# Slopes transformed at another place, conversions two at a time, one PSUM pool: a sparse-attention kernel with two MLP layers on one core

## The chip, the cores and the metric

The kernel runs on one core of a Trainium2 chip. The metric is device time in microseconds (us) of one execution. The engines are named as in the profile: PE (TensorE matmul), PEld (its weight loads), DVE (VectorE), ACT (ScalarE), POOL (GpSimd) and SP (SyncE, which issues nearly all DMAs here; its issues are listed as SPq).

## The reference

Three parts in sequence, all in float32 at the outside:

```
scores = (q @ k^T) / 8              # 4 batches x 8 heads, 576 x 576, head size 64
keep a score if it is >= row maximum - tau, else it counts as -1e9
attn   = exp(scores - max) / sum    # softmax over what is kept
x      = attn @ v                   # heads side by side: 2304 tokens x 512
h      = x @ w_in;  g = max(h, 0) + alpha * min(h, 0);  x = g @ w_out      # layer 1, 512 -> 2048 -> 512
h      = x @ w_in2; g = h > 0 ? h : exp(min(h, 0)) - 1; out = g @ w_out2   # layer 2, same sizes
```

The weights reach the chip as float64 bit patterns (loaded as 64-bit integers) and have to be turned into float32 there. `alpha` holds one slope for each of the 2048 hidden units of layer 1.

## The kernel before

**Stages.** Attention takes the first 364 us of the profiled execution, layer 1 the time from 364 to 778 us, layer 2 the rest. Every matmul of the MLPs works on values split into a high and a low part (`hi`, `lo = x - hi`), three products for one.

**Order of the work.** Every compute instruction goes through `pe`, `dve`, `act` or `pool` (class `Pinned`), which keeps each engine in the order in which the program was written. That order comes from time tables: a step is put down with a due time (`put(at, step)`), all steps are sorted by it and written out (`run`). So a step that waits holds up everything behind it on its engine. In attention the unit of due time is a job (one head's 128 rows of scores; `AT` gives the stages of a job relative to its number), and `beside(i)` is called every 1.3 jobs. In the MLPs the unit is about half an `h` or `o` block of layer 1 (12 matmuls of 128x128 by 128x384), as `sequence` lays them out: a chunk of 384 tokens takes 64 units, `begin` (layer 2's start) is at unit 384.

**Attention.** For each job: scores on PE into a double bank (pool `ps_s`, 3 buffers), row maximum on DVE (`top`), exponential on ACT, masking with the sum on DVE, scaling on POOL, transposes on PE into pool `ps_t` (2 banks), copies out on ACT. `prep(u, i)` transposes the next unit's k and q on PE. Units of q and k are loaded by SP in `load_unit`. Ahead of the first job stand, unpinned, a few DVE instructions: two on `tau` (lines 842 and 843), and line 846, which turns the slopes into 1 - alpha in place after line 845 has loaded them.

**Conversions.** A group (`groups`) is one 128-wide block of a layer-1 weight matrix, or two blocks of a layer-2 matrix (which are also combined into the seven operands of a Strassen-like product and stored to DRAM). `single()` makes one float32 block `x` in three steps: two ACT copies (`x<-r`, `t<-r`), then three DVE operations with a POOL addition at the end (`x<-x,t`). `conversion(g)` continues: for a layer-1 block the high part (from block 10 on ACT, `w<-x`) and the low part (DVE, `w<-x,w`). Both are Python generators; `convert_step` advances the one open conversion by one step. During attention 20 of the 32 layer-1 groups are converted. The other 12, two for each of the blocks 10 to 15, are due during layer 1's first chunk at 0.85 units a step (5 steps a group), and the 16 layer-2 groups (13 steps each) after that, spread evenly up to 8 units before `begin`:

```
    for i in range(4 * KFF):
        put(0.85 * i + 0.45, convert_step, len(groups))
```

**Layer 1.** `hidden_block(c, f)` multiplies (PE into tag `h`, pool `ps_h`, 4 banks), then ACT `t<-psh`, DVE `g<-t,alpha,psh`, ACT `gh<-g`, DVE `gl<-g,gh`. `outer_block` multiplies these two blocks later (LAG = 2) into the four banks of pool `ps_a`. At a chunk's end `result` copies the four banks to tiles `o` (2 buffers), which SP stores to `y`.

**Between the layers.** The last chunk's `outer_block` frees weight tiles in turn: of blocks 0 to 3 for layer 2's weights, of blocks 4 to 9 for its operands (`xs_of`, five 384-column blocks to a tile). `operand_steps(n)` loads `y`, makes the seven operands for each half `kb` of the depth, and splits them. `operand` says in which blocks one operand lies: the two halves of one product side by side. Then the pools `staging` and `first_layer` are closed, and pool `mlp2` (left side of SBUF) and pool `ps_8` (all 8 banks) are opened (lines 900 to 906).

**Layer 2.** `first_product` takes products in `IN_ORDER` 1, 2, 6, 7, 5, 3, 4; the third of them accumulates on the bank of the first, after ACT has copied that out (`keep`, tile `c`). `psum()` hands out banks in rotation over eight.

Of the kernel before, what the change touches and what calls it, by code (L numbers as in the profile page):

```python
# [20 lines left out]
def sparse_attention_two_mlps(  # L21
# [13 lines left out]
    nc = tc.nc  # L35
# [140 lines left out]
    def conversion(g):  # L176
        layer, part, p = group = groups[g]
        if layer == 0:
            for x in single():
                yield  # L180
            if part == 0:
                wt[p] = new_block(p)
            hi, lo = wt[p][:, part, 0, :], wt[p][:, part, 1, :]
            high_of(dve if p < FIRST else act, hi, x)
            if p >= FIRST:
                yield
            difference(dve, lo, x, hi.bitcast(F32))
            stored.add(group)
            return
        xs = []  # L190
        for _ in range(2):
            for x in single():
                yield
            xs.append(x.rearrange("p (a m) -> p a m", a=2))
        (a11, a12), (a21, a22) = [[x[:, h] for h in range(2)] for x in xs]
        if part == 1:
            a12, a21 = a21, a12
        s = stage.tile([P, 4, HM], F32, tag="s", name="s", bufs=1)
        s1, s2, s3, s4 = (s[:, n] for n in (0, 1, 2, 3))
        made = [((1, 2) if part == 0 else (1,), xs[0]), ((4,) if part == 0 else (2, 4), xs[1]),  # L200
                ((5, 6), s[:, 0:2]), ((7, 3), s[:, 2:4])]
        made[1] = (made[1][0], xs[1][:, 2 - len(made[1][0]):2])
        split = {}

        def high(n):
            products, of = made[n]
            split[n] = stage.tile([P, 2, 2, HM], F32R, tag="split", name="split", bufs=2)
            high_of(act, split[n][:, 0:len(products), 0, :], of[:, 0:len(products)])

        def low(n):  # L210
            products, of = made[n]
            many = len(products)
            difference(dve, split[n][:, 0:many, 1, :], of[:, 0:many],
                       split[n][:, 0:many, 0, :].bitcast(F32))

        def store(n):
            for i, product in enumerate(made[n][0]):
                to = in_d[p][:, IN_ORDER.index(product)] if part == 0 else out_d[product - 1][:, p]
                nc.sync.dma_start(out=to, in_=split[n].bitcast(F32)[:, i])
            split.pop(n)  # L220

        total(dve, s1, a21, a22)
        high(0)
        yield
        low(0)
        difference(dve, s2, s1, a11)
        high(1)
        yield
        low(1)
        difference(dve, s4, a12, s2)  # L230
        store(0)
        yield
        difference(dve, s3, a11, a21)
        high(2)
        store(1)
        yield
        low(2)
        high(3)
        yield
        low(3)  # L240
        store(2)
        yield
        store(3)
        stored.add(group)

    converting, started = [], [0]

    def convert_step(limit):
        if not converting and started[0] < min(limit, len(groups)):
            converting.append(conversion(started[0]))  # L250
            started[0] += 1
        if converting and next(converting[0], "end") == "end":
            converting.pop()

    def convert_until(group):
        while group not in stored:
            convert_step(len(groups))


    units_of = [(n, part, i, h) for n in range(NSC) for part in range(2) for i in range((FP, 7)[part]) for h in range(2)]  # L260
# [280 lines left out]

    def operand(product, kb):

        i = 2 * (2 * (product - 1) + kb)
        return xs_of[i], xs_of[i + 1]

    def operand_steps(n):

        for kb in range(2):
            b = {product: operand(product, kb)[1].bitcast(F32) for product in IN_ORDER}  # L550
            for product, kh, th in ((1, 0, 0), (5, 0, 1), (2, 1, 0), (3, 1, 1)):
                nc.sync.dma_start(out=b[product], in_=y_d[2 * n + th][:, 2 * kh + kb, :])
            yield
            for made, first, second in ((7, 3, 5), (5, 5, 1), (6, 3, 5), ("split", 7, None), (4, 2, 6),
                                        *(("split", product, None) for product in (6, 5, 4, 1, 2, 3))):
                if made != "split":
                    t = inp.tile([P, HT], F32, tag="tt", name="tt")
                    difference(dve, t, b[first], b[second])
                    b[made] = t
                else:  # L560
                    hi, lo = operand(first, kb)
                    act.activation(out=hi, in_=b[first], func=AF.Copy)
                    yield
                    difference(dve, lo, b[first], hi.bitcast(F32))
                yield

    gs = {}
    ps_h = []

    def hidden_block(c, f, put, ends):  # L570
        held = {}
        start, done = ends["h", c, f]

        def multiply():
            held["h"] = ps = ps_first[0].tile([P, 512], F32, tag="h", name="psh")[:, 0:HT]
            i = 0
            for kk in range(KDM):
                for wpart, xpart in ((0, 0), (0, 1), (1, 0)):
                    pe.matmul(out=ps, lhsT=wt[f][:, 0, wpart, kk * P:(kk + 1) * P], rhs=ins[c][xpart][:, kk],
                              start=(i == 0), stop=(i == 3 * KDM - 1))  # L580
                    i += 1
# [23 lines left out]
    def outer_block(c, f, put, ends):  # L605
        start, done = ends["o", c, f]

        def multiply():
            if f == 0:
                accs[c] = [ps_first[1].tile([P, 512], F32, tag="a", name="psa")[:, 0:HT] for _ in range(KDM)]  # L610
            hi, lo = gs.pop((c, f))
            for m in range(KDM):
                for i, (wpart, g) in enumerate(((0, hi), (1, hi), (0, lo))):
                    pe.matmul(out=accs[c][m], lhsT=wt[f][:, 1, wpart, m * P:(m + 1) * P], rhs=g,
                              start=(f == 0 and i == 0), stop=(f == KFF - 1 and i == 2))

        def result(m):
            o = mlp.tile([P, HT], F32, tag="o", name="o", bufs=2)
            if m % 2 == 0:
                act.activation(out=o, in_=accs[c][m], func=AF.Copy)  # L620
            else:
                dve.tensor_copy(out=o, in_=accs[c][m])
            nc.sync.dma_start(out=y_d[c][:, m, :], in_=o)
# [9 lines left out]
                put(done + 0.3, add_tile, xs_of, wps[1])  # L633

    def psum():
        return ps_h[0].tile([P, 512], F32, tag="h", name="psh")

    def first_product(n, p, put, ends):

# [72 lines left out]
    def combine(n, p, name):  # L712
        b11, b12, b21, b22 = (gs.get((n, p, kh, th)) for kh in range(2) for th in range(2))
        if name in ("t3", "t2"):
            sums[p, name] = mlp.tile([P, HT], F32, tag=name, name=name, bufs=FP)
        if name == "t3":
            difference(dve, sums[p, name], b22, b12)
        elif name == "t1":
# [25 lines left out]
    def second_product(n, put, ends):  # L744
# [28 lines left out]
            act.activation(out=kept[name, m][:, 0:width(m)], in_=banks[1][m][:, 0:width(m)], func=AF.Copy)  # L773

        def result(fh, th, product, other, m):
            o = mlp.tile([P, 512], F32, tag="o", name="o", bufs=3)
            to = o[:, 0:width(m)]
            total(dve, to, banks[product][m][:, 0:width(m)], kept[other, m][:, 0:width(m)])
            r0 = n * SC + th * HT + 2 * m * P
# [63 lines left out]
    nc.vector.tensor_scalar(out=tau_sb, in0=tau_sb, scalar1=0.0, scalar2=-1.0, op0=ALU.max, op1=ALU.mult)  # L843
    load_values(1)
    nc.sync.dma_start(out=alpha, in_=moe_alpha.rearrange("(f p) -> p f", p=P))
    nc.vector.tensor_scalar(out=alpha, in0=alpha, scalar1=-1.0, scalar2=1.0, op0=ALU.mult, op1=ALU.add)
    for i in range(2):
        load_piece(i)
    for i in range(4):
# [1 line left out]
    first_in = load_in(0)  # L851

    def beside(i):
        if i > 4:
            convert_step(2 * FIRST)
        if i == 78 or i >= 90 and i % 4 == 0:
            next(first_in, None)
# [7 lines left out]
    wps.append(ctx.enter_context(tc.tile_pool(name="wb", bufs=KFF - FIRST, side="right")))  # L865
    inps.append(first_layer.enter_context(tc.tile_pool(name="in1", bufs=1, side="right")))
    mlp = first_layer.enter_context(tc.tile_pool(name="mlp", bufs=1, side="right"))
    ps_first = [first_layer.enter_context(tc.tile_pool(name=name, bufs=4, space=PSUM)) for name in ("ps_h", "ps_a")]

    ends = sequence()  # L870
    for c in range(NCH):
# [9 lines left out]
                put(ends["h", c, 6][0] + 4.05 * i, next, steps, None)  # L881
    begin = ends[0, 0, 0, 1][0]
    for i in range(4 * KFF):
        put(0.85 * i + 0.45, convert_step, len(groups))
    steps = 13 * KFF
    for i in range(steps):
        put(0.85 * 4 * KFF + (begin - 0.85 * 4 * KFF - 8) * i / steps + 0.45, convert_step, len(groups))
    for n in range(NSC):
        for p in range(FP):
            first_product(n, p, put, ends)  # L890
        second_product(n, put, ends)
        steps = operand_steps(n)
        for i in range(38):
            if n == 0:
                put(ends["o", NCH - 1, FIRST - 1][1] + 0.5 + 0.5 * i, next, steps, None)
            else:
                put(ends[n - 1, 0, FP - 1, 4][1] + 0.6 + 1.25 * i, next, steps, None)
    run(begin)
# [1 line left out]
    staging.close()  # L900
    first_layer.close()
    mlp = ctx.enter_context(tc.tile_pool(name="mlp2", bufs=1))
    for _ in range(KFF - FIRST):
        add_tile(gs_of, wps[2])
    gs_of.tiles.append(mlp.tile([P, 2 * HT], F32R, tag="g", name="g"))
    ps_h.append(ctx.enter_context(tc.tile_pool(name="ps_8", bufs=8, space=PSUM)))
    run(float("inf"))
# [1 line left out]
_INS = ['q', 'k', 'v', 'tau', 'moe_w_in', 'moe_w_out', 'moe_alpha', 'moe2_w_in', 'moe2_w_out']  # L909
# [26 lines left out]
```

## Time and profile before

| | |
|---|---|
| median of 3 runs | 1145.3 us (1144.07 to 1145.32) |
| profiled execution, its own time | 1144.36 us |
| its span, first to last instruction | 1142.6 us |
| busy share of the span: PE / PEld / DVE / ACT / POOL | 96 / 83 / 70 / 60 / 23 % |
| chain that ended last: PE / ACT / DVE / issue / POOL | 79 / 7 / 6 / 3 / 2 % |
| mean granted PE clock | 0.992 of full |

Busy time is that of one profiled execution; the ends of matmuls in it are modelled, so a short PE stall costs somewhat more than the idle time that is listed for it. What an engine waited for ("idle before", with a releaser) is inferred from semaphore events. The chain that ended last is followed back from the last instruction.

### The profile page before, as it was taken

Reading aid. Unit: us, or ns where it says so; the run is one execution under the profiler, and the core shown is the slowest. Engines: PE = TensorE matmul, PEld = TensorE weight load, DVE = VectorE, ACT = ScalarE, POOL = GpSimd, SP = SyncE. Lnnn points to the kernel's source line nnn. Section 1 sums busy time; section 2 is a strip of 40 time slices with the busy share of each in tenths; the row PEclk is TensorE's granted clock in tenths of the full one; section 3 lists DMA queues with packets and bytes.
Section 4 is the critical chain, followed back from the end, with each engine's and each line's share of the span. In section 5 each row is a group of like instructions: output and inputs, shape, how many; then the busy total and the mean of one; then the engine's idle time right before and its main releaser. Section 6 shows DMA issues by size and latency. Waiting matters only on the chain.

```text
span 1142.6 us, 20027 instructions
## 1 busy us (share of the span) xinstructions
PE 1093.8 (96%) x7016; PEld 946.8 (83%) x7016; DVE 794.3 (70%) x1639; ACT 686.9 (60%) x1421; POOL 268.1 (23%) x438
## 2 busy tenths in 40 slices
PE   3999999999998998999999999999999999999998
PEld 2555555555555987999999999998999999999998
DVE  2888887888884676656656655675788578857765
ACT  2787777777775545444444443455776467656653
POOL 0666656666663221101111011000000000000000
PEclk8999999999999999999999999999999999999999
DMA  5343444444222335453454534833698868786774
GB/s 135 90 123 89 127 114 104 110 106 105 72 59 82 96 95 189 150 187 128 147 194 139 205 126 152 292 130 131 256 328 259 255 250 328 266 276 242 256 264 163
DMA packets 149156, 194.79 MB, mean 170 GB/s; under 512 B 85824, under 2 KB 117056, under 8 KB 140608
## 3 DMA queue, kind: packets, MB, share of 16 engines
q1 hardware_dynamic: 149056, 193.51, 52.7%
q8 instruction: 56, 0.92, 0.3%
q14 instruction: 44, 0.36, 0.1%
HBM read 149.96 MB, written 43.52 MB: 169 GB/s over the span
## 4 chain that ended last, share of the span: by engine, by line
PE 79%; ACT 7%; DVE 6%; issue 3%; POOL 2%; SPq 2%; DMA 1%; DVEq 0%; POOLq 0%; ACTq 0%
PE psh L93 46%; PE psa L93 15%; PE pst L93 14%; PE ps L93 5%; ACT e L93 2%; ACT pt L93 2%; POOL x L93 2%; DVE x L93 1%; DVE st L93 1%; DVE e L93 1%; DVE w L93 1%; ACT t L93 1%; ACT w L93 1%; ACT x L93 0%; SPq L304 0%
## 5 line engine op out<-in xcount | busy, mean ns | idle before, releaser
L93 PE MATMUL psh<-ih,w 128*128 128x384 f32 x768 | 210.3, 337 | 0.0
L93 PE MATMUL psa<-gh,w 128*128 128x384 f32 x768 | 197.1, 338 | 4.9 <-ACT gh L93 4.9
L93 PE MATMUL psh<-w,th 128*128 128x256 f32 x1008 | 183.0, 283 | 0.0
L93 PE MATMUL psh<-w 128*128 128x384 f32 x1008 | 176.8, 334 | 2.4 <-ACT o L93 2.2
L93 PEld LDWEIGHTS psh<-w 128*128 128x128 f32 x1008 | 174.3, 188 | 3.3 <-ACT o L93 2.5
L93 POOL TENSOR_TENSOR x<-x,t 128x512 uint32<-128x512 uint32 x64 | 84.6, 1321 | 338.1 <-DVE x L93 322.0
L93 PEld LDWEIGHTS psh<-w,th 128*128 128x128 f32 x1008 | 157.7, 192 | 0.0
L93 PEld LDWEIGHTS psa<-gh,w 128*128 128x128 f32 x768 | 138.9, 188 | 7.1 <-ACT gh L93 6.8
L93 PE MATMUL psh<-w,tl 128*128 128x256 f32 x504 | 143.1, 284 | 0.6 <-DVE tl L93 0.6
L93 PEld LDWEIGHTS psh<-ih,w 128*128 128x128 f32 x768 | 140.5, 188 | 0.1
L93 DVE TENSOR_REDUCE st<-ps 128x1 f32<-128x576 f32 x144 | 108.1, 751 | 37.9 <-PE ps L93 37.2
L93 PE MATMUL psa<-gl,w 128*128 128x384 f32 x384 | 130.6, 340 | 1.8 <-DVE gl L93 1.8
L93 PEld LDWEIGHTS pst<-ident,e 128*128 128x128 f32 (+1 forms) x720 | 74.6, 137 | 68.8 <-issue 32.5
L93 PE MATMUL psh<-il,w 128*128 128x384 f32 x384 | 129.1, 336 | 0.0
L93 DVE SCALAR_TENSOR_TENSOR e<-ps,st,e 128x576 f32<-128x576 f32 x144 | 116.7, 811 | 13.1 <-POOL st L93 7.5
L93 POOL TENSOR_SCALAR e<-e,st 128x576 f32<-128x576 f32 x144 | 116.4, 812 | 30.9 <-DVE st L93 21.4
L93 ACT ACTIVATE e<-ps,st 128x576 f32<-128x576 f32 x144 | 107.0, 743 | 26.0 <-DVE st L93 25.0
L93 PE MATMUL ps<-kt,qt 64*128 64x288 f32 (+1 forms) x640 | 111.8, 457 | 11.2 <-DVE e L93 11.2
L93 PE MATMUL pst<-ident,e 128*128 128x128 f32 (+1 forms) x720 | 114.9, 285 | 6.1 <-issue 1.7
L93 ACT ACTIVATE pt<-pst 128x512 f32<-128x512 f32 (+2 forms) x240 | 109.6, 464 | 16.7 <-PE pst L93 15.0
L93 ACT ACTIVATE t<-psh 128x384 f32<-128x384 f32 x120 | 58.0, 484 | 86.9 <-PE psh L93 86.2
L93 DVE SCALAR_TENSOR_TENSOR g<-t,alpha,psh 128x384 f32<-128x384 f32 x96 | 58.8, 612 | 57.5 <-ACT t L93 57.2
(81 smaller groups left out, 1642.8 us busy)
## 6 DMA issues: line engine op xcount, KB each, us to landing
w<-wo SPq DMA_DIRECT2D x42, 1024.0 KB, 6.1
w<-wi SPq DMA_DIRECT2D x24, 1024.0 KB, 6.6
w<-wi SPq DMA_DIRECT2D x24, 768.0 KB, 4.4
r<-in_moe_w_in_dram SPq DMA_DIRECT2D x32, 512.0 KB, 3.7
r<-in_moe_w_out_dram SPq DMA_DIRECT2D x32, 512.0 KB, 3.6
wi<-split SPq DMA_DIRECT2D x56, 256.0 KB, 2.3
wo<-split SPq DMA_DIRECT2D x56, 256.0 KB, 2.3
qr<-in_q_dram SPq DMA_DIRECT2D x64, 128.0 KB, 2.6
```

What stands on the lines that cost most here:

```text
L93: return lambda *args, **named: tc.keep_in_program_order(made(*args, **named))
```

## The change

Five edits. (1) The line that turns the slopes into 1 - alpha leaves its place ahead of attention (unpinned, DVE) and is written at the fifth call of `beside`, on POOL and in order. (2) A conversion now says at each step how far it is (0: no block yet, 1: the first of two, 2: all its blocks taken), and `convert_step` may keep two open (in the MLPs; still one in attention): the second starts when the first has state 2, and the calls alternate between them, but an open conversion in state 1 waits until the older one has ended. Each call still advances one step. The layer-2 groups are now due up to 24 units before `begin` instead of 8. (3) One PSUM pool `ps_all` with tags `h` and `a`, four banks each, serves both layers; `psum()` takes four of the one, then four of the other. (4) Tiles: layer 1's `o` gets 3 buffers; layer 2's `t3`, `t2`, `o` and the last `g` tile move to a new pool `late` on the right side of SBUF. (5) The operands of depth half `kb` lie together (first half in the tiles freed by blocks 4 to 6, second in those of 7 to 9), their steps start when those tiles are free instead of after block 9, at 0.7 instead of 0.5 units a step, and products are split in the order 1, 7, 2, 6, 5, 3, 4.

```
-                yield
+                yield 2 if x is not None else 0
...
-                yield
+                yield len(xs) + (x is not None)
...
-    converting, started = [], [0]
-
-    def convert_step(limit):
-        if not converting and started[0] < min(limit, len(groups)):
-            converting.append(conversion(started[0]))
+    converting, started, turn = [], [0], [0]
+
+    def convert_step(limit, together=1):
+
+        if (started[0] < min(limit, len(groups)) and len(converting) < together
+                and all(state == 2 for _, state in converting)):
+            converting.append([conversion(started[0]), 0])
             started[0] += 1
-        if converting and next(converting[0], "end") == "end":
-            converting.pop()
+        if converting:
+            turn[0] += 1
+            one = converting[-1 if turn[0] % 2 and converting[-1][1] != 1 else 0]
+            one[1] = next(one[0], None)
+            if one[1] is None:
+                converting.remove(one)
...
     def operand(product, kb):
-        i = 2 * (2 * (product - 1) + kb)
+        i = 3 * PER * kb + 2 * (product - 1)
         return xs_of[i], xs_of[i + 1]
...
-            for made, first, second in ((7, 3, 5), (5, 5, 1), (6, 3, 5), ("split", 7, None), (4, 2, 6),
-                                        *(("split", product, None) for product in (6, 5, 4, 1, 2, 3))):
+            for made, first, second in ((7, 3, 5), (5, 5, 1), (6, 3, 5), ("split", 1, None), ("split", 7, None),
+                                        (4, 2, 6), *(("split", product, None) for product in (2, 6, 5, 3, 4))):
...
-            held["h"] = ps = ps_first[0].tile([P, 512], F32, tag="h", name="psh")[:, 0:HT]
+            held["h"] = ps = ps_all.tile([P, 512], F32, tag="h", name="psh")[:, 0:HT]
...
-                accs[c] = [ps_first[1].tile([P, 512], F32, tag="a", name="psa")[:, 0:HT] for _ in range(KDM)]
+                accs[c] = [ps_all.tile([P, 512], F32, tag="a", name="psa")[:, 0:HT] for _ in range(KDM)]
...
-            o = mlp.tile([P, HT], F32, tag="o", name="o", bufs=2)
+            o = mlp.tile([P, HT], F32, tag="o", name="o", bufs=3)
...
     def psum():
-        return ps_h[0].tile([P, 512], F32, tag="h", name="psh")
+        given[0] += 1
+        return ps_all.tile([P, 512], F32, tag="ha"[given[0] // 4 % 2], name="psh")
...
-    nc.vector.tensor_scalar(out=alpha, in0=alpha, scalar1=-1.0, scalar2=1.0, op0=ALU.mult, op1=ALU.add)
...
     def beside(i):
+        if i == 4:
+            pool.tensor_scalar(out=alpha, in0=alpha, scalar1=-1.0, scalar2=1.0, op0=ALU.mult, op1=ALU.add)
         if i > 4:
             convert_step(2 * FIRST)
...
-    ps_first = [first_layer.enter_context(tc.tile_pool(name=name, bufs=4, space=PSUM)) for name in ("ps_h", "ps_a")]
+    ps_all = ctx.enter_context(tc.tile_pool(name="ps_all", bufs=4, space=PSUM))
...
-        put(0.85 * i + 0.45, convert_step, len(groups))
+        put(0.85 * i + 0.45, convert_step, len(groups), 2)
     steps = 13 * KFF
     for i in range(steps):
-        put(0.85 * 4 * KFF + (begin - 0.85 * 4 * KFF - 8) * i / steps + 0.45, convert_step, len(groups))
+        put(0.85 * 4 * KFF + (begin - 0.85 * 4 * KFF - 24) * i / steps + 0.45, convert_step, len(groups), 2)
...
-                put(ends["o", NCH - 1, FIRST - 1][1] + 0.5 + 0.5 * i, next, steps, None)
+                put(ends["o", NCH - 1, RING + 2 + 3 * (i // 19)][1] + 0.5 + 0.7 * (i % 19), next, steps, None)
...
     mlp = ctx.enter_context(tc.tile_pool(name="mlp2", bufs=1))
+    late = ctx.enter_context(tc.tile_pool(name="late", bufs=1, side="right"))
...
-    gs_of.tiles.append(mlp.tile([P, 2 * HT], F32R, tag="g", name="g"))
-    ps_h.append(ctx.enter_context(tc.tile_pool(name="ps_8", bufs=8, space=PSUM)))
+    gs_of.tiles.append(late.tile([P, 2 * HT], F32R, tag="g", name="g"))
```

## Rows read from the trace of the kernel before

**Rows 1.** Windows by stage: length, then busy time and instructions of PE, PEld, DVE, ACT, POOL

```profile
364.17:443.14 78.97, 72.30 (x387) 67.47 (x386) 52.40 (x97) 39.88 (x79) 19.32 (x14) 0.99 0.41 127
443.14:510.71 67.57, 67.57 (x385) 67.15 (x385) 42.15 (x82) 32.33 (x65) 8.53 (x6) 0.99 0.48 167
577.66:644.30 66.64, 66.64 (x386) 66.64 (x385) 41.53 (x83) 31.79 (x64) 9.35 (x7) 1.00 0.47 162
```

**Rows 2.** Timeline of the start: start, duration, engine, operation, idle before and its releaser

```profile
11.40 2.29 PE L93 MATMUL ps<-kt,qt 64*128 64x288 f32 x8
13.88 1.14 SPq L307 DMA_DIRECT2D qr<-in_q_dram  x2
19.48 0.59 SPq L845 DMA_DIRECT2D alpha<-in_moe_alpha_dram  x1
22.91 0.17 DVE L846 TENSOR_SCALAR alpha<-alpha 128x16 f32<-128x16 f32 x1 [18.96 <-DMA alpha<-in_moe_alpha_dram]
23.00 0.75 DVE L93 TENSOR_REDUCE st<-ps 128x1 f32<-128x576 f32 x1
25.62 1.33 PE L93 MATMUL ps<-kt,qt 64*128 64x288 f32 x4 [9.40 <-DVE e L93]
26.88 1.11 PE L93 MATMUL pst<-ident,qr 128*128 128x128 f32 x4
```

**Rows 3.** The page's DMA issues: operation, count, KB each, us from issue to landing

```profile
qr<-in_q_dram SPq DMA_DIRECT2D x64, 128.0 KB, 2.6
```

**Rows 4.** PE's waits in attention, 30 to 340 us, the longest: total, times, longest

```profile
PE pst L93 <- ACT pt L93: 9.2, 23, 1.1
```

**Rows 5.** PE's waits around layer 1's first chunk, 345 to 445 us

```profile
PE psa L93 <- ACT gh L93: 4.9, 6, 1.6
```

**Rows 6.** Chain that ended last, one conversion's turn in the first chunk: start, duration

```profile
389.91 1.54 POOL x L93
...
391.48 0.64 ACT w L93
...
392.14 0.69 DVE w L93
...
394.18 0.70 DVE x L93
...
395.03 1.54 POOL x L93
```

**Rows 7.** Timeline of conversions' operations on POOL and DVE, first chunk

```profile
405.28 1.44 POOL L93 TENSOR_TENSOR x<-x,t 128x512 uint32<-128x512 uint32 x1 [3.61 <-DVE x L93]
...
431.40 0.88 DVE L93 TENSOR_SCALAR x<-x 128x512 f32<-128x512 f32 x2
433.18 1.27 POOL L93 TENSOR_TENSOR x<-x,t 128x512 uint32<-128x512 uint32 x1 [4.85 <-DVE x L93]
433.45 1.74 DVE L93 TENSOR_SCALAR x<-x 128x512 f32<-128x512 f32 x2
```

**Rows 8.** Timeline of the change from layer 1 to layer 2

```profile
779.57 0.56 DVE L93 COPY o<-psa 128x384 f32<-128x384 f32 x1 [2.00 <-DMA y<-o]
780.23 2.32 PE L93 MATMUL psh<-w 128*128 128x384 f32 x12 [2.21 <-ACT o L93]
782.19 0.49 ACT L93 ACTIVATE c<-psh 128x384 f32<-128x384 f32 x1 [2.70 <-DMA y<-o]
782.74 17.43 PE L93 MATMUL psh<-w 128*128 128x384 f32 x99 [0.18 <-ACT c L93]
```

**Rows 9.** Timeline of the change from attention to layer 1

```profile
364.17 0.58 PE L93 MATMUL psh<-ih,w 128*128 128x384 f32 x1
364.61 0.44 ACT L93 ACTIVATE xt<-pst 128x320 f32<-128x320 f32 x1 [2.87 <-PE pst L93]
371.40 0.44 PE L93 MATMUL psa<-gl,w 128*128 128x384 f32 x1 [0.17 <-DVE gl L93]
```

**Rows 10.** Groups by shape: conversions' split copies, count, busy, mean ns, idle before

```profile
L93 ACT ACTIVATE split<-s 128x512 fp32r<-128x512 f32 x32 | 20.0, 625 | 20.6 <-DMA wi<-split 10.4 <-DMA wo<-split 9.3 <-DVE g L93 0.7
```

More of the change, by code (lines that the diff above doesn't have):

```diff
@@ L185, in conversion @@
             if p >= FIRST:
-                yield
+                yield 2
             difference(dve, lo, x, hi.bitcast(F32))
@@ L192, in conversion @@
             for x in single():
-                yield
+                yield len(xs) + (x is not None)
             xs.append(x.rearrange("p (a m) -> p a m", a=2))
@@ L223, in conversion @@
         high(0)
-        yield
+        yield 2
         low(0)
@@ L227, in conversion @@
         high(1)
-        yield
+        yield 2
         low(1)
@@ L231, in conversion @@
         store(0)
-        yield
+        yield 2
         difference(dve, s3, a11, a21)
@@ L235, in conversion @@
         store(1)
-        yield
+        yield 2
         low(2)
         high(3)
-        yield
+        yield 2
         low(3)
         store(2)
-        yield
+        yield 2
         store(3)
         stored.add(group)
-    converting, started = [], [0]
-    def convert_step(limit):
-        if not converting and started[0] < min(limit, len(groups)):
-            converting.append(conversion(started[0]))
-            started[0] += 1
-        if converting and next(converting[0], "end") == "end":
-            converting.pop()
+    converting, started, turn = [], [0], [0]
[3 more added lines that the diff above has]
+            converting.append([conversion(started[0]), 0])
+            started[0] += 1
+        if converting:
[4 more added lines that the diff above has]
+                converting.remove(one)
     def convert_until(group):
         while group not in stored:
-            convert_step(len(groups))
+            convert_step(len(groups), 2)
     units_of = [(n, part, i, h) for n in range(NSC) for part in range(2) for i in range((FP, 7)[part]) for h in range(2)]
@@ L567, in sparse_attention_two_mlps @@
     gs = {}
-    ps_h = []
+    given = [-1]
     def hidden_block(c, f, put, ends):
@@ L714, in combine @@
         if name in ("t3", "t2"):
-            sums[p, name] = mlp.tile([P, HT], F32, tag=name, name=name, bufs=FP)
+            sums[p, name] = late.tile([P, HT], F32, tag=name, name=name, bufs=FP)
         if name == "t3":
@@ L775, in result @@
         def result(fh, th, product, other, m):
-            o = mlp.tile([P, 512], F32, tag="o", name="o", bufs=3)
+            o = late.tile([P, 512], F32, tag="o", name="o", bufs=3)
             to = o[:, 0:width(m)]
```

## The prediction

> **What bounds the kernel now.** The page first: PE is busy for 1093.8 of 1142.6 us, so a gain has to come out of the 49 us in which it is not, or from matmuls at a lower clock. Next the table of windows, cut by stage and chunk. A chunk of layer 1 with nothing in its way takes 66.64 us and PE is busy in all of it. The first chunk takes 78.97 us for the same number of matmuls, PE is idle for 6.67 us of it, and the second takes 67.57 [rows 1]. Third, the timeline of the start: DVE runs nothing from 4 us until 22.91, where line 846 ends a wait of 18.96 us for the slopes, and only then comes the first row maximum [rows 2]. PE, which has its first scores from 11.40 on, stops when its three score buffers are full and waits 9.40 us [rows 2]. Fourth, the change of layers: PE stands still for 2.21 us and then waits 0.18 us more [rows 8]. These are three places where PE waits for something that is no matmul, and the change touches all three. In the rest of layers 1 and 2 PE's windows are full; attention is full but for small waits, the longest entry 9.2 us over 23 waits, and none of them is for a DMA [rows 4].
>
> **The slopes.** The DMA of the slopes is issued at 19.48, behind the loads of the first two units on SP, and line 846 is ahead of the first maximum on DVE. Without it the first maximum can start when the first half of the eight score matmuls is done: 11.40 + 2.29/2 = 12.55, some 0.1 later, instead of 23.00 [rows 2], so 10.4 us earlier. What is late next is the second unit's q: PE's order puts its transposes (26.88) between the fourth and fifth job's scores. That load is issued as a pair from 13.88, the second about 14.45; it lands 2.6 us later [rows 3], so at 17.1, or 17.7 if the first unit's 3.8 us from issue to use is repeated. The transposes then run at 17.1 to 17.7 instead of 26.88: 9.2 to 9.8 us earlier. Loads of later units wait for buffers that PE's transposes free, so they move with PE; and no wait of PE from 30 us on is for a load [rows 4]. So the lead is kept through attention; that loads have room for it is read from the missing wait alone, which is why its opposite is a rival below. PE's score matmuls after its long idle time ran at 1.2 GHz (1.33 us for four at 25.62 [rows 2], the pace of its first ones); an earlier start could give back up to 1 us of that, which I leave out. On POOL the operation costs 0.17 us if as on DVE [rows 2], at most about 1; POOL meets it some nine jobs into attention, after the data, and is busy for only 23 % of the span. **I take 9.4, bounds 8.5 to 10.4.** If attention were paced by its loads, it would be as little as 3.
>
> **Two conversions at a time.** In the first chunk the due times ask for a group every 5 x 0.85 units, and a unit is 66.64/64 = 1.04 us: 4.43 us. One conversion alone can't keep that: its turn is POOL 1.54, ACT high 0.64, DVE low 0.69, the next block's two DVE steps 0.88 [rows 7], a slope operation or gl of layer 1 0.4, DVE 0.70, small gaps: 395.03 - 389.91 = 5.12 us [rows 6]. So it falls back by 0.69 us a group. The eighth POOL addition was due at 364.17 + 1.04 x (0.85 x 37 + 0.45) = 397.4, about 398.4 with its DVE step, and ran at 405.28 [rows 7]: nearly 7 us late, and just there PE begins to wait for gh and gl, which stand behind the conversion on ACT and DVE [rows 5]. So about 6 us of delay is free, the rest goes to PE. The first chunk costs 78.97 - 66.64 = 12.33 us more than a clean one, and the second 0.93 more, its first matmuls at the lower of the two clock levels after the waits (granted 0.99) [rows 1]: 13.3 us to be had.
>
> With two open, the steps of two groups take ten calls as before (8.86 us), but between a POOL addition and the ACT step that needs it there is now, for every other group, a call of the other conversion. The chain over two groups becomes ACT high 0.64, ACT's two copies of the next block 1.1, its DVE steps 0.88 and 0.70, POOL 1.3 to 1.5, ACT high 0.64, DVE low 0.69, DVE 0.70, POOL 1.3 to 1.5: 8.0 to 8.4 us, with layer 1's operations in it about 9 to 9.5, against 10.24. It falls back by 0.1 to 0.6 us in two groups, at most 4 in all six pairs: less than the 6 that are free. I leave 2 us of the 13.3 for a few waits, **and take 11.3, bounds 5 (a chain of 9.9 us and half the waits) to 13.**
>
> A rule speaks against this. POOL's addition took 1.27 us alone; the DVE pair that began 0.27 us after it (433.45) took 1.74 instead of 0.88, ending 0.74 after POOL did [rows 7]. The Trainium skill, SBUF — State Buffer, section "SBUF: two separate sides", says that VectorE and GpSimd share a port pair by an exclusive lock: whichever starts first holds it for its whole instruction and the other blocks. By that rule, which the trace agrees with, the interleaving makes the case common that was rare. Priced with the rows: if each of two groups lost the 0.86 on the chain, the pair would take about 11, worse than 10.24, and the gain would be nil. I don't take that value, since the pair that is pushed back by the lock then has the other group's high and low steps to wait for anyway (it would end at POOL's end + 0.74, the low step starts at POOL's end + 0.7). It is the first rival.
>
> In the later chunks PE waits for nothing, so 16 groups interleaved have nothing to give; ACT, 48 % busy there, and DVE, 62 %, hide them [rows 1]. If that cover went, it would be the third rival.
>
> **One PSUM pool, `o`, `late`, operands.** At 780.23 PE's first product of layer 2 starts 0.1 after DVE has copied out the last bank of layer 1 (779.57 + 0.56), although it writes a bank of the `h` tag that was read long ago; and the copy `c` at 782.19 waits 2.70 for a store of `o` [rows 8]. Both are the first tile of a new pool waiting for all that the old pool held. With one pool, and `mlp2` now over conversion tiles that are long free, the product starts at 778.02: 2.21 less, and the 0.18 at 782.74 go. The fifth bank, still to be copied out at 779.6, is wanted some five products (5.2 us) later. A third `o` saves ACT a wait off PE's path. Operands split in the last 5 us before layer 2 now end earlier, and PE didn't wait for them. `late` is first written some 9 us into layer 2, after the last store. **I take 2.2, bounds 1.5 to 2.4.**
>
> The same pool has a price at the other end: `ps_all` lies over all eight banks, so over the two of `ps_t` as well, whose last reader is ACT's copy `xt`, 364.61 + 0.44. By the same pattern layer 1's first matmul moves from 364.17 to about 365.15 [rows 9], 0.98 us; the 0.17 at 371.40 [rows 9] goes in return. **I take -0.8, bounds -1.0 to -0.2.**
>
> **Sum.** 9.4 + 11.3 + 2.2 - 0.8 = 22.1 us off the profiled execution's own 1144.36 (span 1142.6 and 1.76 around it): 1122.3. That execution lies 0.94 under the median of the runs shown, so I say 1123.2. All best bounds together: 25.6 less, 1119.7; all worst: 14.0 less, 1131.3.
>
> **Rivals.**
> - *The interleaving gives nothing* (the port lock, or order on ACT). For: the 1.74 [rows 7], and that half the groups still have the ACT step right behind the addition. Against: the chain above. 10.8 less: 1134.5.
> - *Attention takes the lead back*: loads, not DVE, pace the first units. For: the slopes' place behind loads that land late [rows 2]. Against: no wait for a load after 30 us [rows 4]. The slopes give 3: 1129.6.
> - *Slower*: with two layer-2 groups open, ACT's split copies wait for stores while gh stands behind them. Before, 32 such copies waited 19.7 us for stores [rows 10] at no cost to PE, as about 6 us of delay is free. It decides only if single waits pass 6 us; at 1.8 us of PE for each of 16 groups, 29 us, it would end at 1152.
> - *No effect*: the slopes' place and the pool change are undone by an order that I have misread. About 1145.
>
> **How the numbers follow.** The forecast (1119 to 1131) 0.78, no interleaving gain 0.08, lead lost 0.07, slower 0.04, no effect 0.03. Range 1118 to 1132, which leaves out most of the first rival and the last two. A change within 0.2 % (2.3 us) can't be told from none: faster 0.93, same 0.03, slower 0.04.
>
> **What would show it.** Right: the first row maximum near 12.7 us and layer 1 about 8.6 earlier; the first chunk at 67 to 69 us with hardly a wait for gh or gl, the second at 66.7; a wait of about 1 us of PE for `xt` at layer 1's start; layer 2's first matmul right behind layer 1's last. Wrong: a second unit whose q lands later than 18 us, DVE's shift pairs at 1.7 with the first chunk still above 75, or new PE waits in chunks two to six.

## The result: 14 us faster, and the profile after

The changed kernel takes 1130.83 us (median of four runs, 1130.32 to 1131.58) against 1144.91 (four runs, 1144.07 to 1145.32): ratio 0.9878, 95% interval 0.9861 to 0.9896. The profiled execution's span goes from 1142.6 to 1129.4. Cut at PE's own instructions in both timelines, the 13.2 us lie here:

| stretch | before, us | after, us | difference |
|---|---|---|---|
| start to the last value matmuls of attention | 361.46 | 351.37 | -10.09 |
| from there to layer 1's first matmul | 2.71 | 3.64 | +0.93 |
| first chunk of layer 1 | 78.97 | 77.32 | -1.65 |
| second chunk | 67.57 | 67.97 | +0.40 |
| third chunk to layer 2's first product | 269.52 | 267.44 | -2.08 |
| layer 2 to the end | 362.37 | 361.66 | -0.71 |

The windows of the first two chunks and of a later one, in the columns of [rows 1]:

```profile
355.01:432.33 77.32, 71.07 (x385) 68.01 (x385) 54.55 (x97) 42.19 (x82) 20.08 (x15) 0.98 0.41 125
432.33:500.30 67.97, 67.34 (x386) 66.72 (x386) 42.99 (x85) 31.95 (x65) 8.53 (x7) 1.00 0.51 174
567.00:633.70 66.70, 66.70 (x386) 66.70 (x385) 44.89 (x88) 32.17 (x66) 9.89 (x7) 1.00 0.49 166
```

PE stands still in the first chunk for 6.25 us; before, it was 6.67. The interleaving was to take nearly all of that. PE's waits from 345 to 445 us (the first line stands for the 4.9 of [rows 5]):

```profile
PE psa L93 <- ACT gh L93: 5.6, 6, 2.0
...
PE psa L93 <- DVE gl L93: 1.1, 2, 0.7
PE psh L93 <- ACT xt L93: 0.5, 1, 0.5
```

At the start the first row maximum no longer stands behind the slopes, and the second unit's q is transposed at 17.69 (for 26.88 in [rows 2]). Timelines of DVE and of PE:

```profile
12.78 0.76 DVE L93 TENSOR_REDUCE st<-ps 128x1 f32<-128x576 f32 x1 [8.85 <-PE ps L93]
```
```profile
17.69 1.11 PE L93 MATMUL pst<-ident,qr 128*128 128x128 f32 x4
```

At the change of layers PE goes on without a gap (layer 2's first matmul starts 0.17 us behind layer 1's last, the usual distance), while the copies of `o` still run; in [rows 8] it waited 2.21 and 0.18 us:

```profile
767.57 0.34 PE L93 MATMUL psa<-gl,w 128*128 128x384 f32 x1
...
767.74 3.48 PE L93 MATMUL psh<-w 128*128 128x384 f32 x19
768.90 0.56 DVE L93 COPY o<-psa 128x384 f32<-128x384 f32 x1 [1.45 <-DMA y<-o]
769.00 0.49 ACT L93 ACTIVATE c<-psh 128x384 f32<-128x384 f32 x1 [1.09 <-PE psh L93]
```

What holds the first chunk is seen where PE's waits begin (the first is at 403.83). One turn of a pair of conversions in the timelines of ACT, DVE and POOL:

```profile
403.69 0.67 ACT L93 ACTIVATE x<-r 128x512 f32<-128x512 f32 x1
404.26 0.65 ACT L93 ACTIVATE t<-r 128x512 uint32<-128x512 uint32 x1
407.05 0.63 ACT L93 ACTIVATE w<-x 128x512 fp32r<-128x512 f32 x1 [2.14 <-POOL x L93]
407.59 0.47 ACT L93 ACTIVATE t<-psh 128x384 f32<-128x384 f32 x1
408.74 0.52 ACT L93 ACTIVATE gh<-g 128x384 fp32r<-128x384 f32 x1 [0.68 <-DVE g L93]
412.97 0.63 ACT L93 ACTIVATE w<-x 128x512 fp32r<-128x512 f32 x1 [3.71 <-POOL x L93]
```
```profile
404.88 0.69 DVE L93 SCALAR_TENSOR_TENSOR x<-r,x 128x512 uint32<-128x512 uint32 x1
408.10 0.61 DVE L93 SCALAR_TENSOR_TENSOR g<-t,alpha,psh 128x384 f32<-128x384 f32 x1 [2.53 <-ACT t L93]
408.63 0.88 DVE L93 TENSOR_SCALAR x<-x 128x512 f32<-128x512 f32 x2
...
410.49 0.69 DVE L93 SCALAR_TENSOR_TENSOR x<-r,x 128x512 uint32<-128x512 uint32 x1
```
```profile
405.73 1.29 POOL L93 TENSOR_TENSOR x<-x,t 128x512 uint32<-128x512 uint32 x1 [5.31 <-DVE x L93]
411.65 1.29 POOL L93 TENSOR_TENSOR x<-x,t 128x512 uint32<-128x512 uint32 x1 [4.63 <-DVE x L93]
```

Read it as a ring. ACT's high step `w` (407.05) stands in ACT's order directly behind the other block's copies, and waits 2.14 us for POOL. Layer 1's `t` stands behind it, DVE's `g` behind `t`, and behind `g` the other block's shift pair (the two DVE operations on `x`, 408.63), although its input was ready at 403.69 + 0.67 = 404.36. So POOL's next addition comes 5.92 us after the last, where the due times, at a clean chunk's pace, ask for 4.43. The other block's high step (412.97) then stands behind its own addition with no call in between, and ACT is idle for 3.71 us.

A second thing shows at the chunk's end. ACT's timeline there:

```profile
420.98 0.69 ACT L93 ACTIVATE x<-r 128x512 f32<-128x512 f32 x1 [1.35 <-DMA r<-in_moe_w_in_dram]
...
425.69 0.67 ACT L93 ACTIVATE x<-r 128x512 f32<-128x512 f32 x1 [1.88 <-DMA r<-in_moe_w_in_dram]
```

and in the chain that ended last (start, duration):

```profile
417.16 3.74 DMA r<-in_moe_w_in_dram
420.98 0.51 ACT x L93
421.49 4.12 DMA r<-in_moe_w_in_dram
425.69 0.67 ACT x L93
```

These are pieces of layer 2: the second of its first group, and the first of its second group, which begins as soon as the first has both. All pieces go through the same two buffers in turn, and ACT waits for the loads with gh behind. PE's longest wait, 1.96 us (it ends at 428.54), follows, and after it the lower clock level (1.2 GHz) for some 3 us, in which a pair of matmuls took 0.84 instead of 0.51. The window of that stretch, with a granted clock of 0.53:

```profile
428.50:431.50 3.00, 2.96 (x9) 2.77 (x10) 2.95 (x7) 0.78 (x2) 0.00 (x0) 0.53 0.05 19
```

### The profile page after: what moved, and what is told of

Read it like the earlier page. It is cut to its first block, busy times and chain, and to the rows that moved or that the text cites. A ratio compares the mean times of both kernels' runs of the same rounds, so it can differ in the third digit from the quotient of the medians.

```text
span 1129.4 us, 20026 instructions
## 1 busy us (share of the span) xinstructions
PE 1091.4 (97%) x7016; PEld 946.5 (84%) x7016; DVE 801.6 (71%) x1638; ACT 688.0 (61%) x1421; POOL 269.5 (24%) x439
## 4 chain that ended last, share of the span: by engine, by line
PE 79%; ACT 7%; DVE 6%; issue 3%; POOL 2%; DMA 1%; SPq 1%; DVEq 0%; POOLq 0%; ACTq 0%
PE psh L93 45%; PE psa L93 15%; PE pst L93 14%; PE ps L93 4%; ACT e L93 3%; ACT pt L93 2%; DVE x L93 1%; DVE e L93 1%; DVE st L93 1%; POOL x L93 1%; ACT t L93 1%; DVE g L93 1%; ACT x L93 1%; DMA r<-in_moe_w_in_dram 1%; DVE w L93 1%
## 5 line engine op out<-in xcount | busy, mean ns | idle before, releaser
L93 DVE SCALAR_TENSOR_TENSOR e<-ps,st,e 128x576 f32<-128x576 f32 x144 | 116.7, 811 | 12.7 <-POOL st L93 7.4
```

Source lines behind the costliest of these rows:

```text
L93: return lambda *args, **named: tc.keep_in_program_order(made(*args, **named))
```

## The experiments

Each time is a median, beside the kernel before on the same chip (1144.9 to 1145.3 in the three batches, so kernels of different batches are compared directly below). "Changed kernel" is the one of the diff; a difference without another name is against it or, for slopes_alone and pools_alone, against the kernel before. Of most edits only the deciding lines are shown, and `...` marks what is left out.

**slopes_alone**: the kernel before with the slopes' operation moved to POOL in `beside`.

> The kernel before with the slopes' move alone. Reading of the two traces: the lead of attention is 10.1 us (its last value matmuls begin at 351.37 instead of 361.46), and all else is as before, so 10.1 us less than before, about 1134.8, with layer 1's first matmul near 354.1 (no wait for xt, since the two PSUM pools are those of before). Rival: part of the changed kernel's lead comes from elsewhere or is given back in layer 1; then less than 8 us.

1135.38 us, ratio 0.9911 (0.9896 to 0.9926): 9.9 less. Attention's last value matmuls come at 352.02, 9.44 earlier, and PE still waits at the change of layers (2.22 us for `o`, until 770.61). The lead is kept.

**one_conversion**: the changed kernel, `convert_step` called for one conversion at a time.

```
-        put(0.85 * i + 0.45, convert_step, len(groups), 2)
+        put(0.85 * i + 0.45, convert_step, len(groups))
...
```

> The changed kernel with one open conversion at a time in the MLPs again, all other edits kept. If the interleaving brings what the two traces show (the first chunk 77.3 instead of 79.0 us, the second 68.0 instead of 67.6), this is 1 to 2 us slower than the changed kernel, about 1132. Rival, the forecast's own size: the interleaving does save some 11 us and another edit takes them back; then this is about 1142.

1133.54 us, ratio 0.9896 (0.9880 to 0.9913). So the interleaving gives 2.7 us where 11.3 were forecast. In the middle of the first chunk POOL's additions are 5.12 apart, as before. That chunk takes 77.43 us here (355.36 to 432.79) and 77.32 in the changed kernel, so by these two traces almost nothing of the 2.7 lies where the forecast had it; it lies in the later chunks.

**sum_unread**: the changed kernel, the addition's result not read by anything; the low bits of those weights are left out.

```
-        pool.tensor_tensor(out=bits, in0=bits, in1=t, op=ALU.add)
+        pool.tensor_tensor(out=t if i >= 2 * FIRST else bits, in0=bits, in1=t, op=ALU.add)
```

> The changed kernel, with POOL's addition in the MLPs writing over its second operand, which nobody reads, instead of the block (the low bits of those weights are left out). POOL does the same work at the same time, but ACT's high step no longer waits for it. Theory order (ACT's high step waits for POOL, and layer 1's t, g, gh and gl stand behind it on ACT and DVE): PE's waits in the first chunk fall from 6.7 to under 3 us, 5 to 9 us faster than the changed kernel, 1122 to 1126. Rival lock (DVE's operations are blocked while POOL adds, so DVE and POOL together are too slow for the due times): within 2 us of the changed kernel. Rival loads: the part up to 415 us goes (some 4 us), the waits at the chunk's end stay.

1123.93 us, ratio 0.9812 (0.9797 to 0.9828): 6.9 less than the changed kernel. POOL's and DVE's work is all there, and with it any contention between them (a shift pair beside an addition still takes 1.83 us, at 373.53); only the waits for POOL's result are gone. POOL's timeline and PE's waits:

```profile
377.23 1.56 POOL L93 TENSOR_TENSOR t<-x,t 128x512 uint32<-128x512 uint32 x1 [2.62 <-DVE x L93]
381.41 1.56 POOL L93 TENSOR_TENSOR t<-x,t 128x512 uint32<-128x512 uint32 x1 [2.62 <-DVE x L93]
```
```profile
PE psa L93 <- ACT gh L93: 1.8, 1, 1.8
```

Here a group takes 4.18 us. Of the waits one is left, and it lies in the second chunk (it ends at 430.71), where `g` stands on DVE behind a copy of `o` that waits 4.63 us for a store. The wait for POOL in ACT's order is a cause, and the theory of contention falls. ACT also waits for pieces of layer 2 at the first chunk's end here (1.27 and 1.65 us), and PE does not wait: where no delay has built up, those loads cost PE nothing.

**layer2_later**: the changed kernel, layer 2's groups begun only behind the first chunk.

```
-    for i in range(4 * KFF):
-        put(0.85 * i + 0.45, convert_step, len(groups), 2)
-    steps = 13 * KFF
+    for i in range(60):
+        put(0.85 * i + 0.45, convert_step, 2 * KFF, 2)
+    steps = 13 * KFF + 4
...
```

> The changed kernel, with the conversions of layer 2's weights kept out of the first chunk: 60 calls for the 12 groups of layer 1, the others from 2 units after that chunk on. Theory loads (at the end of the first chunk ACT waits for raw blocks whose two buffers are reloaded too late, 1.35 and 1.88 us, and gh stands behind it; then a stretch at the lower clock): PE's waits from 420 us on go, 3 to 5 us faster than the changed kernel, about 1127. Theory order alone: the delay that has built up until then stays and is paid at the chunk's end by other waits; under 2 us.

1126.09 us, ratio 0.9831 (0.9817 to 0.9846): 4.7 less. PE's waits for gh go from 5.6 to 2.3, the longest 0.8, and the second chunk to 66.64. The early groups of layer 2 are the second cause; the waits that remain lie at 403 to 421.

**newest_next**: layer2_later and one line, so that the call behind every POOL addition goes to the other block.

```
             started[0] += 1
+            turn[0] = 0
```

> layer2_later (1126.09) with one line more: when a conversion is begun, the next call goes to it. So in every group, not only in every other one, a call to the other conversion stands between POOL's addition and ACT's high step that waits for it. Order theory (ACT, in order, waits at the high step with layer 1's t and gh behind it): the waits of the layer 1 stretch 403 to 421 (gh 2.3, gl 1.1 in layer2_later) go down to under 1 us in all, and 2.5 to 4 us of the time: 1122 to 1123.6. Rival (the first chunk is late from the amount of work that ACT and DVE have there, load_in(1)'s operations among it): the waits only move, 1125 to 1127.

1120.22 us, ratio 0.9785 (0.9771 to 0.9800): 5.9 less than layer2_later, under the range expected. No wait of PE for gh or gl is left. ACT's timeline, and the windows of the first two chunks:

```profile
382.54 0.64 ACT L93 ACTIVATE w<-x 128x512 fp32r<-128x512 f32 x1 [0.24 <-POOL x L93]
383.08 0.47 ACT L93 ACTIVATE t<-psh 128x384 f32<-128x384 f32 x1
...
386.77 0.64 ACT L93 ACTIVATE w<-x 128x512 fp32r<-128x512 f32 x1 [0.25 <-POOL x L93]
```
```profile
355.14:421.99 66.85, 66.85 (x383) 66.85 (x384) 51.21 (x85) 38.01 (x74) 17.02 (x12) 1.00 0.41 123
421.99:488.55 66.56, 66.56 (x385) 66.56 (x385) 45.85 (x86) 33.03 (x67) 10.81 (x8) 1.00 0.48 159
```

From 380 to 390 the changed kernel's high steps waited 1.78, 0.24 and 1.36 us for POOL; here none waits more than 0.25. Later in the chunk they wait up to 2.88 us (411.91) here too, but by then the conversions are less late, and it reaches PE no more. The first chunk is about as long as any other, with all twelve groups in it: the amount of work was no bound.

**newest_gap**: newest_next with an empty call ahead of the high step, so six calls to a group, at 5/6 of the distance.

> newest_next with six calls for a group in place of five (one idle call between POOL's addition and the high step) at five sixths of the pace, so that the groups come as often as before. Order theory: two calls of the other conversion now stand between the addition and the high step, 1.4 to 2.1 us; POOL is never waited for by layer 1's t or gh; the first chunk comes within 1 us of the second one (66.6): 1120 to 1122.5. Rival (amount of work): as newest_next within 0.5 us. If the empty call only delays a group (its low step and the next group's start are later), slower than newest_next by up to 2 us.

1120.34 us (0.9771 to 0.9804), the same as newest_next: PE has nothing more to gain there, so this run does not tell the two theories apart.

**newest_slower**: newest_next, calls 0.98 apart.

> newest_next with the 60 calls of layer 1's groups 0.98 apart in place of 0.85 (the last at 58.3 units in place of 50.6, still before its block is read). Order theory: the steps are queued by place, not by time; a pace slower by 15% leaves 0.13 more for each call, so newest_next's remaining waits shrink by up to 1 us: 1121 to 1123. Rival (amount of work in the first chunk): the same operations spread over 15% more time take away most of the waits by themselves: 1120 to 1121.5, and the gain over newest_next is then more than newest_next's own over layer2_later.

1120.14 us (0.9770 to 0.9800), the same again. It lies in the rival's range, but not on the rival's ground: the pace gave nothing over newest_next, whose order had already taken away all the waits.

**two_pools**: layer2_later with two lasting PSUM pools.

```
...
-    ps_all = ctx.enter_context(tc.tile_pool(name="ps_all", bufs=4, space=PSUM))
+    ps_all, ps_a = (ctx.enter_context(tc.tile_pool(name=name, bufs=4, space=PSUM)) for name in ("ps_h", "ps_a"))
```

> layer2_later with the one PSUM pool (tags h and a) made two pools of four banks each (ps_h, ps_a), both kept to the end, layer 2 taking from them in turn. If the wait at the change from attention to layer 1 (first matmul 0.53 behind ACT's last xt) is the price of one pool over all eight banks, that wait goes, the first matmul follows the last value matmul by 0.1 to 0.3 us, and layer 2's start keeps its own gain: 0.8 to 1.0 less than 1126.09, about 1125.2. Rival: layer 1's start is bound by something else there (its operands, or the lead is lost in the first chunk's waits): no change, 1125.8 to 1126.4.

1126.17 us (0.9823 to 0.9852), as layer2_later. The wait for `xt` is gone: from the last value matmuls to layer 1's first matmul 2.70 us (352.85 to 355.55) instead of 3.64. The first chunk is about 1 us longer (73.7 against 72.6 in layer2_later), so nothing of it reaches the end.

**two_newest**: two_pools with newest_next's line.

> two_pools with the line of newest_next. In two_pools the first matmul of layer 1 came 0.9 earlier behind attention's last value matmuls, but the first chunk took 0.9 longer, since its waits for POOL didn't come earlier. With those waits gone the lead should stay: 0.9 less than newest_next, 1119.1 to 1119.5. If it is lost again (something else in the first chunk or at layer 2's start holds the end), 1120.0 to 1120.5.

1120.03 us (0.9767 to 0.9794). Against newest_next's 1120.22, no difference that these runs can tell; they can't tell 0.9 from none either, so whether the lead is kept here stays open.

**after_newest**: the changed kernel with newest_next's line alone.

> The changed kernel (1130.83) with the one line of newest_next alone: the next call goes to a conversion just begun. Layer 2's groups still come behind layer 1's in the first chunk. If the order of the high step and layer 2's raw loads are two causes side by side, this gives the order's part, 4 to 6 us, and the waits for raw loads at the first chunk's end stay: 1125 to 1127. If the order is the root of both (the high steps held ACT so long that the raw loads came late too), nearly all of newest_next's gain is here: 1120 to 1122.

1125.98 us (0.9816 to 0.9843): 4.8 less than the changed kernel, though its four runs are spread widest (1123.60 to 1127.27). Two waits for gh are left: 1.46 at 423.14, after ACT waited 1.44 for a piece of layer 2, and 1.81 at 433.80, where `g` stands on DVE behind a copy of `o` that waits for a store:

```profile
431.10 0.56 DVE L93 COPY o<-psa 128x384 f32<-128x384 f32 x1 [4.61 <-DMA y<-o]
```

That store is issued on SP behind the split stores of layer 2's first groups (the first of the chunk's four at 426.52); without such groups they are issued from 421.33 and the same copy waits 1.45 (newest_next). Order and early groups of layer 2 are two causes side by side: 4.8 and 4.7 alone, 10.6 together.

**one_later**: layer2_later, one conversion at a time.

> layer2_later with one conversion at a time. Against newest_next (1120.22) it measures what two conversions at a time are worth where ACT's order doesn't hold them up. The forecast's term was 11.3 us: if it was right but for the order, 1130 to 1133 (each of the twelve groups again takes a turn of some 5.1 us, and all high steps wait for POOL). If two conversions are worth only what one_conversion against the changed kernel showed (2.7), 1123 to 1127.

1128.02 us (0.9838 to 0.9865): between the two expectations. In newest_next's order two conversions at a time are worth 1128.02 - 1120.22 = 7.8 us; in the order of the change, 1128.02 - 1126.09 = 1.9, and again not in the first chunk (72.65 here, 72.61 in layer2_later). In the middle of that chunk POOL's additions are again 5.12 apart. All six kernels side by side, in us:

| | layer 2's groups due as in the change | begun behind the first chunk |
|---|---|---|
| one conversion at a time | 1133.54 | 1128.02 |
| two, in the order of the change | 1130.83 | 1126.09 |
| two, with a call in between in every turn | 1125.98 | 1120.22 |

The first row says more: the early groups cost 5.5 us with one conversion at a time as well. So that price was not made by keeping two groups open, and the kernel before has such groups in its first chunk too.

**pools_alone**: the kernel before with the parts of the diff for the pool, `o`, `late` and the operands.

> The kernel before with the PSUM pool of both layers, three o tiles, the late pool, and layer 2's operands in the new order and at the new times; slopes and conversions as before. The forecast's terms: 2.2 gained at the change to layer 2, 0.8 lost at layer 1's start. If both count, 1.4 less than before, 1143.5; if the loss at layer 1's start falls into the first chunk's waits as two_pools suggests, 2.2 to 2.8 less, 1142.1 to 1142.7. If the gain at layer 2's start needs the other parts of the change, no difference.

1141.15 us, ratio 0.9963 (0.9950 to 0.9977): 4.0 less, more than any of the expectations said. Its trace is 3.3 shorter. Of that, 2.3 lie between the third chunk's start and layer 2, and 0.7 in layer 2. Nothing is lost before: layer 1 starts 1.03 later than in the kernel before (365.20), but its third chunk starts at 510.40, where it stood at 510.71.

```profile
365.20 0.44 PE L93 MATMUL psh<-ih,w 128*128 128x384 f32 x1 [0.53 <-ACT xt L93]
```
```profile
365.20:443.12 77.92, 71.65 (x384) 67.32 (x385) 52.40 (x97) 39.38 (x78) 19.27 (x14) 0.99 0.41 127
```

## Why the prediction came out as it did

The mechanisms at the start and at the change of layers were right; the largest term was not. It came out at 2.7, under its own lower bound of 5, and the first chunk at 77.3, where the prediction asked for 67 to 69. That 1130.83 still lies inside the forecast (1119 to 1131), just under its end, is luck: pools and slopes brought more than was said and made up for a part.

- **Slopes: right.** 9.4 forecast; 10.1 in the trace, 9.9 timed alone. The first maximum came at 12.78 (12.65 said), the second unit's q at 17.69 (17.1 to 17.7 said, 9.19 earlier), and attention kept it all. The rival of a lead taken back falls. The rest of the lead is there at the third unit's q (24.40 for 34.35, 9.95 earlier). By its place it is the clock, which the prediction named and left out. From 25.60 to 30.00 the kernel before had a granted clock of 0.50, the lower level, after PE's 9.40 us of waiting; the changed kernel has 1.00 from 8.47 to 30.00. One reading beside it was wrong: the first score matmuls, at 11.40, had 1.00 in both kernels, so the four at 25.62 did not run at the pace of the first ones.
- **Two conversions: the step that failed.** 11.3 forecast, 2.7 timed (one_conversion). The failing sentence is "It falls back by 0.1 to 0.6 us in two groups, at most 4 in all six pairs". From the first addition to the twelfth the due times, at a clean pace, ask for 11 x 4.43 = 48.7 us. It took 59.64 in the kernel before, 60.13 in one_conversion and 59.97 in the changed kernel: two at a time, in the order of the change, were no faster than one, and fell back by 11 us. In newest_next it took 53.15, which is 4.4 behind. The first and the twelfth addition on POOL's timeline, in the kernel before, the changed kernel and newest_next:

```profile
367.40 1.29 POOL L93 TENSOR_TENSOR x<-x,t 128x512 uint32<-128x512 uint32 x1 [11.51 <-ACT t L93]
...
427.04 1.29 POOL L93 TENSOR_TENSOR x<-x,t 128x512 uint32<-128x512 uint32 x1 [3.95 <-DVE x L93]
```
```profile
357.30 1.29 POOL L93 TENSOR_TENSOR x<-x,t 128x512 uint32<-128x512 uint32 x1 [11.53 <-DVE x L93]
...
417.27 1.28 POOL L93 TENSOR_TENSOR x<-x,t 128x512 uint32<-128x512 uint32 x1 [4.33 <-DVE x L93]
```
```profile
357.43 1.29 POOL L93 TENSOR_TENSOR x<-x,t 128x512 uint32<-128x512 uint32 x1 [11.53 <-DVE x L93]
...
410.58 1.29 POOL L93 TENSOR_TENSOR x<-x,t 128x512 uint32<-128x512 uint32 x1 [2.63 <-DVE x L93]
```

  Between 364.76 and 387.86 two groups of the changed kernel did take 9.4 to 9.9 us, nearly as worked out, and then 10.3 to 12.7. Four of its additions in between, two groups apart:

```profile
364.76 1.29 POOL L93 TENSOR_TENSOR x<-x,t 128x512 uint32<-128x512 uint32 x1 [6.16 <-DVE x L93]
...
374.27 1.53 POOL L93 TENSOR_TENSOR x<-x,t 128x512 uint32<-128x512 uint32 x1 [4.37 <-DVE x L93]
...
383.63 1.54 POOL L93 TENSOR_TENSOR x<-x,t 128x512 uint32<-128x512 uint32 x1 [3.60 <-DVE x L93]
...
393.88 1.44 POOL L93 TENSOR_TENSOR x<-x,t 128x512 uint32<-128x512 uint32 x1 [4.50 <-ACT x L93]
```

  The sum of the chain put layer 1's operations in as a filling of about 1 us. They are links: half of the high steps still stood directly behind their addition, as the prediction itself noted, and each held up `t`, `g` and the other block's next steps for two engines. newest_next, which changes only that order, confirms it, and there the forecast's own 4 us of falling back nearly came true.
- **What was not seen**: that the first groups of layer 2 begin inside the first chunk. "16 groups interleaved have nothing to give" was argued from chunks where PE waits for nothing. But twelve groups of five steps take 60 of the 64 calls; the last four calls, and those of the next series that are due before unit 64, go to layer 2. Its pieces land 3.7 to 4.1 us after issue, and its stores go ahead of layer 1's. layer2_later shows the price, 4.7 us. The kernel before has them there too: the addition at 433.18 in [rows 7] belongs to layer 2.
- **The amount to be had was right, but not what it was for.** "13.3 us to be had": from one_conversion (1133.54) to newest_next (1120.22) it is 13.3 us. Of these, 5.5 are the early groups of layer 2 and 7.8 the two conversions with the order mended, so the term of 11.3 could not have come true even with the right order. The change took 2.7.
- **The port lock** was rightly not priced on the path. In newest_next a shift pair beside an addition still takes 1.89 us instead of 0.88 (DVE's timeline below), and five of the twelve pairs take 1.48 to 1.98, where the kernel before has 0.88 or 0.89 for all twelve; yet the chunk is clean. The stretched pair agrees with the rule of the lock in the Trainium skill, SBUF — State Buffer, section "SBUF: two separate sides". It costs no time that shows here. The rival named "the port lock, or order on ACT" was right in its second half.

```profile
377.15 1.89 DVE L93 TENSOR_SCALAR x<-x 128x512 f32<-128x512 f32 x2
```

- **Pools, tiles and operands: right in place, small in size.** 2.2 forecast, 2.8 in the trace (2.08 up to layer 2's start, 0.71 in layer 2), 4.0 timed alone; where the 0.7 in layer 2 comes from is not shown. The price at layer 1's start was there in place and size (0.93, forecast 0.8), but pools_alone and two_pools show that it doesn't reach the end: the first chunk runs to ACT's and DVE's pace, and a later start only waits less. In this kernel it should have been taken as 0.
- **Slower through waits for stores** and **no effect**: neither showed in the time, though a wait for a store did hold PE up for 1.8 us in sum_unread and in after_newest. By the trace the sum of 22.1 misses by +0.7 at the slopes, +0.6 at the pools, -0.1 at the price and -10.05 at the conversions: 13.2. The 1.25 us that the first two chunks lost there are not surely the interleaving's: pools_alone, with one conversion at a time, has 145.20 for the two chunks, the changed kernel 145.29.

What stays open: slopes alone, pools alone and the step from one_conversion to the changed kernel give 9.9 + 4.0 + 2.7 = 16.6 us, and the change 14.1. If the gap is real, it lies before the interleaving, since one_conversion, which has the first two parts, gives 11.8 and not 13.9; it also has layer 2's groups due earlier (24 instead of 8 units before `begin`), and no run changes that number alone. With intervals of some 1.5 us on each the gap may also be nothing. Single traces differ by as much: attention is the same work in the changed kernel and in the ten that are made from it, and its last value matmuls start between 351.30 and 352.92.

newest_next, at 1120.22 us, beats the kernel before by 24.7 us and the changed kernel by 10.6.

## What to carry to other kernels

When two pieces of work are interleaved on engines that run in order, don't add up durations: write down what stands behind each waiting instruction on its engine, and check that the order put something else between an operation and the one that waits for it, in every turn and not in every other one. A stage that gets faster brings the next stage's loads forward; look for what they meet. And when a stretch is paced by other engines, a later start of PE alone costs nothing there (pools_alone), and an earlier one gains nothing (two_pools).

## What the runs showed of the hardware

A wait of PE can cost more than its length. In the changed kernel's first chunk the longest wait (1.96 us) was followed by 3 us at a granted clock of 0.53, with 9 matmuls where a clean chunk has 17: some 1.4 us more, by that estimate. That chunk was 10.7 us over a clean one (66.64) though PE was idle for only 6.25 of it; the rest of the difference lies in matmuls around the waits, whose ends are modelled. Not every wait brings the lower level: behind the 2.21 us at the change of layers the kernel before had a granted clock of 1.00 (780.23 to 785.00).
